# Even/odd partition runs, a zero-weighted fifth tile, another order for batch 0 and held-back weights in a linear-attention and expert-layer kernel

## The chip, the cores and the metric

The kernel runs on one core of one Trainium2 chip. The metric is the device time of one execution in microseconds (us). Every kernel was executed several times; the record marks each execution as fast or slow, and all executions told here are fast ones.

Engine names in the profile: PE is the TensorE matmul, PEld its weight load, DVE is VectorE, ACT is ScalarE, POOL is GpSimd, SP issues DMA (the copies between the chip's main memory and its on-chip memory). PEclk is the granted share of TensorE's clock.

## The reference

Eight batches, eight heads, 576 tokens of 64 features go through a linear attention with cosine weights; its output feeds an expert layer of two matmuls with `h * cos(h)` between them. All inputs and outputs are float32. The text calls phi(q) and phi(k) below the q and k features.

```python
def _attn_ref(q, k, v):                      # (8, 8, 576, 64) each
    theta = np.pi / 2.0 * pos / S
    phi(x) = concatenate([relu(x) * cos(theta), relu(x) * sin(theta)], -1)
    kv  = einsum('bhsf,bhsd->bhfd', phi(k), v);   z = sum(phi(k), axis=2)
    num = einsum('bhsf,bhfd->bhsd', phi(q), kv)
    den = einsum('bhsf,bhf->bhs',  phi(q), z) + 1e-06
    return num / den

def _moe_ref(x, w_in, w_out):                # x: (4608, 512), w_in: (512, 2048)
    h = x @ w_in
    return (h * cos(h)) @ w_out
```

## The kernel before

576 tokens are 4 tiles of 128 and a remainder of 64. One half of the partitions holds runs of 5 consecutive tokens, the other half runs of 4; even and odd batches swap the halves, so that two batches' remainders share one tile later. Remainders live in tiles of their own. `n` is the parity of the batch; `KPR`, `V1R` and `QPR` are the remainder's k features, v and q features.

```python
    def half(n):
        return slice(R * n, R * (n + 1))                 # R = 64
    # ... cut ...
        nc.sync.dma_start(
            out=m[half(n)], in_=s_[:, 0:S5, :].rearrange("h (p t) d -> p h t d", t=NT + 1))
        nc.sync.dma_start(
            out=m[half(1 - n), :, 0:NT, :],
            in_=s_[:, S5:S, :].rearrange("h (p t) d -> p h t d", t=NT))
    # ... cut ...
    def prep_v(b):                                       # the "V cast"
        nc.vector.tensor_copy(                           # 4 tiles
            out=V1[b % 2][:, :, :, 0:D],
            in_=m[:, :, 0:NT, :].rearrange("p h t d -> p t h d"))
        nc.vector.tensor_copy(out=V1R[b % 2][hf, :, 0:D], in_=m[hf, :, NT, :])
    # ... cut: kv_group = the KV matmuls, q_trans, num (x = num/den), x_trans ...
    for name in ("k", "v", "q"):
        load(0, name)
    # ... cut ...
    nc.gpsimd.tensor_copy(out=w_in_sb[0:1, 0, 0:1], in_=raw[("v", 0)][0:1, 0, 0, 0:1])
    for g in range(4):
        fs = slice(g * Dff // 4, (g + 1) * Dff // 4)
        nc.gpsimd.dma_start(out=w_in_sb[:, :, fs], in_=wi[:, :, fs])
    for f in attention(0, after=w_in_sb[0:1, 0, Dff // 2:Dff // 2 + 1]):
        f()
    # ... cut: the same for w_out, one element copied from v of batch 1 ...
    for s in range(B + 1):                               # expert of s beside attention of s + 1
        spread(mlp(s), attention(s + 1) if s + 1 < B else [])
```

The one-element copy into `w_in_sb` makes the DMA that overwrites that element wait until v has landed. It overlaps only the first of four pieces: in the timeline below three go out at 6.44 us, and the held one at 24.90, after the copy at 24.43. The order of the source is not the order on the engine: there, w_out's third piece (L340) goes out at 23.64, ahead of the held piece of w_in (L334).

## Time and profile before

| | before |
|---|---|
| time, median of 3 (the record has a fourth, 352.44, which makes the median 353.22) | 353.27 us (353.17 to 353.39) |
| span of the profiled run | 351.6 us |
| PE busy | 305.9 us (87%) |
| first matmul with w_in ("first expert matmul") | 43.35 us |
| KV matmuls of batch 1 start | 49.53 us |
| first output block (first matmul with w_out) | 78.73 us |

The page's second part gives busy tenths in 40 slices of 8.8 us. PE is at 9 from the ninth slice on; only the start has room.

```profile
PE   0034477799999999999999999999999999999993
```

The chain of waits, in order of time (start, duration, what), shows what the start consists of: a wait for w_in, then the V cast and the q features of batch 1, and from 78.89 on TensorE alone.

```profile
24.90 18.31 DMA w_in_sb<-in_moe_w_in_dram
43.35 1.87 PE M_362 L237 x4
45.21 1.69 PE M_374 L237 x4
48.26 1.23 DVE V_1_76 L118
54.26 2.39 DVE qp_352 L100 x6
...
78.89 3.45 PE M_806 L261 x16
```

The timeline of GpSimd shows why the first piece of w_in is the last to come: three other pieces of w_in and two of w_out are issued at 6.4 to 10.3 us, and the held one only at 24.90, behind a third piece of w_out. It was not v that held it so long: VectorE casts the last of that v at 15.94. GpSimd first stood 12.86 us at the copy that holds back k of batch 1, which by the code waits for the third piece of w_in (the profile itself names no releaser for this wait).

```profile
6.44 2.36 POOL L334 DMA_DIRECT2D w_in_sb<-in_moe_w_in_dram  x3
8.77 1.51 POOL L340 DMA_DIRECT2D w_out_sb<-in_moe_w_out_dram  x2
...
23.15 0.39 POOL L84 CAST km_124<-w_in_sb 1x1 f32<-1x1 f16 x2 [12.86 <-issue]
23.64 0.75 POOL L340 DMA_DIRECT2D w_out_sb<-in_moe_w_out_dram  x1
24.43 0.18 POOL L331 CAST w_in_sb<-vm_86 1x1 f16<-1x1 f32 x1
24.90 0.75 POOL L334 DMA_DIRECT2D w_in_sb<-in_moe_w_in_dram  x1 [0.30 <-POOL w_in_sb L331]
```

The tables of windows give, after the stretch and its length, busy time and instructions of PE, PEld, DVE, ACT and POOL, then the granted clock, the busy share of the 16 DMA engines (over 1 where packets overlap) and GB/s written. With loads of k, q, v alone (4 to 10 us) the rate is 211; with loads and weights together (14 to 24) it is 248, of which the loads have 123 (1.23 MB in 10 us, DMA view); with weights alone (24.5 to 26.5) it is 206, for which twice as many bytes are read, since the weights are cast from 4 to 2 bytes on the way (the page counts 36.74 MB read: 28.3 of q, k and v, and 8.4 of weights, which are written as 4.2).

```profile
4.00:10.00 6.00, 0.00 (x0) 0.00 (x0) 0.78 (x2) 2.30 (x3) 5.92 (x10) 1.00 1.14 211
...
14.00:24.00 10.00, 2.36 (x40) 2.23 (x40) 1.71 (x2) 1.38 (x3) 0.72 (x3) 1.00 1.17 248
```

```profile
24.50:26.50 2.00, 1.33 (x13) 1.34 (x14) 1.77 (x4) 2.00 (x4) 1.45 (x4) 1.00 1.24 206
```

### The profile page before, as it was taken

How to read it: one execution, taken by the hardware profiler on the slowest of the kernel's cores; microseconds unless marked ns; L12 is line 12 of the kernel's file. 1: busy time of each engine (PE TensorE's matmuls, PEld its weight loads, DVE VectorE, ACT ScalarE, POOL GpSimd, SP SyncE). 2: the span in 40 equal slices, each digit the busy share in tenths (PEclk: the TensorE clock that was granted, in tenths of full speed). 3: DMA queues.
4: the chain of work that ended last, by engine and by line, in shares of the span. 5: the costliest groups of instructions: out<-in, count | busy, mean ns of one | idle time of the engine just before them, and what ended most of it. 6: DMA issues, size and time to landing. Idle time of an engine off the chain costs nothing.

```text
span 351.6 us, 6070 instructions
## 1 busy us (share of the span) xinstructions
PE 305.9 (87%) x2448; PEld 170.8 (49%) x2448; DVE 202.8 (58%) x491; ACT 185.4 (53%) x284; POOL 13.3 (4%) x30
## 2 busy tenths in 40 slices
PE   0034477799999999999999999999999999999993
PEld 0034235445565555445574554455655554446441
DVE  0421849989996669438784887445943471444100
ACT  1335437665755575356764665557555753555210
POOL 9120010000000000000000000000000000000000
PEclk9998589989999999999999999999999999999999
DMA  7999999829998578940993168202021020220232
GB/s 152 224 235 248 250 200 237 149 58 209 202 203 170 135 163 158 204 122 10 238 196 85 34 132 184 72 2 62 1 47 44 2 62 0 60 49 13 68 83 60
DMA packets 33083, 42.37 MB, mean 121 GB/s; under 512 B 1824, under 2 KB 30496, under 8 KB 33056
## 3 DMA queue, kind: packets, MB, share of 16 engines
q1 hardware_dynamic: 28544, 37.75, 50.3%
q0 software_dynamic: 4224, 4.19, 7.1%
q8 instruction: 19, 0.31, 0.4%
q10 hardware_dynamic: 288, 0.04, 0.1%
q14 instruction: 8, 0.07, 0.1%
HBM read 36.74 MB, written 9.44 MB: 131 GB/s over the span
## 4 chain that ended last, share of the span: by engine, by line
PE 79%; DMA 5%; issue 5%; DVE 4%; ACT 2%; POOL 1%; POOLq 0%
DMA w_in_sb<-in_moe_w_in_dram 5%; ACT ch L229 1%; PE M_4128 L261 1%; PE M_4109 L261 1%; PE M_4049 L261 1%; PE M_2824 L261 1%; PE M_2741 L261 1%; PE M_2601 L261 1%; PE M_2250 L261 1%; PE M_1948 L261 1%; PE M_1815 L261 1%; PE M_1732 L261 1%; PE M_1592 L261 1%; PE M_1454 L261 1%; PE M_1241 L261 1%
## 5 line engine op out<-in xcount | busy, mean ns | idle before, releaser
L237 PEld LDWEIGHTS <-w_in_sb 128*128 128x128 f16 x512 | 47.2, 99 | 48.6 <-issue 7.6
L129 PE MATMUL KV_0_136<-V_0_75,kp_110 128*128 128x65 f16 x16 | 1.2, 243 | 17.3 <-DVE V_0_75 L118 17.3
L249 PEld LDWEIGHTS <-w_in_sb 128*128 128x128 f16 x256 | 14.8, 98 | 0.2
L129 PEld LDWEIGHTS <-kp_110 128*128 128x128 f16 x32 | 2.2, 131 | 17.3 <-issue 17.3
L261 PEld LDWEIGHTS <-g_3761 128*128 128x128 f16 x64 | 6.2, 97 | 7.6
L261 PEld LDWEIGHTS <-g_3287 128*128 128x128 f16 x64 | 6.2, 98 | 7.3
L261 PEld LDWEIGHTS <-g_751 128*128 128x128 f16 x64 | 6.2, 98 | 7.1
L261 PEld LDWEIGHTS <-g_1760 128*128 128x128 f16 x64 | 6.2, 98 | 7.1
L261 PEld LDWEIGHTS <-g_2769 128*128 128x128 f16 x64 | 6.2, 98 | 7.1
L261 PEld LDWEIGHTS <-g_2278 128*128 128x128 f16 x64 | 6.1, 98 | 7.1
L261 PEld LDWEIGHTS <-g_1269 128*128 128x128 f16 x64 | 6.1, 98 | 7.1
L261 PEld LDWEIGHTS <-g_361 128*128 128x128 f16 x64 | 6.1, 98 | 7.1
L142 PEld LDWEIGHTS <-qp_111 128*128 128x128 f16 x32 | 3.3, 148 | 5.6 <-ACT qp_111 L98 5.6
L142 PE MATMUL QP_0_184<-IDENT,qp_111 128*128 128x128 f16 x8 | 1.0, 311 | 5.5 <-ACT qp_111 L98 5.5
L183 PE MATMUL XP_0_304<-IDENT,x_0_254 128*128 128x128 f16 x4 | 0.7, 301 | 5.5 <-DVE x_0_254 L174 5.5
L100 DVE TENSOR_SCALAR KPR_78<-km_124,CS 64x512 f16<-64x512 f32 x2 | 0.9, 487 | 7.8 <-DMA km_124<-in_k_dram 7.8
L98 ACT ACT_TABLE_LOAD x1 | 1.3, 1283 | 7.2 <-DMA km_83<-in_k_dram 7.2
L100 DVE TENSOR_SCALAR qp_1753<-qm_1483,CS 128x512 f16<-128x512 f32 x8 | 3.7, 461 | 1.9 <-PE QP_3_1486 L142 1.9
L230 DVE TENSOR_TENSOR g_3761<-M_3762,ch 128x512 f16<-128x512 f32 x1 | 0.7, 692 | 6.9 <-ACT ch L229 6.9
L237 PE MATMUL M_362<-xT_113,w_in_sb 128*128 128x512 f16 x4 | 1.9, 622 | 3.0 <-DMA w_in_sb<-in_moe_w_in_dram 3.0
L100 DVE TENSOR_SCALAR qp_2762<-qm_2492,CS 128x512 f16<-128x512 f32 x8 | 3.7, 461 | 1.3 <-PE QP_3_2495 L142 1.3
L98 ACT ACTIVATE qp_111<-qm_89,CS 128x512 f16<-128x512 f32 x4 | 2.6, 711 | 3.1 <-DMA qm_89<-in_q_dram 3.1
(1128 smaller groups left out, 864.6 us busy)
## 6 DMA issues: line engine op xcount, KB each, us to landing
out_dram<-ost SPq DMA_DIRECT2D x32, 256.0 KB, 3.2
w_in_sb<-in_moe_w_in_dram POOLq DMA_DIRECT2D x4, 512.0 KB, 16.8
w_out_sb<-in_moe_w_out_dram POOLq DMA_DIRECT2D x4, 512.0 KB, 17.5
out_dram<-ostr SPq DMA_DIRECT2D x8, 128.0 KB, 2.3
km_83<-in_k_dram SPq DMA_DIRECT2D x1, 640.0 KB, 6.4
vm_86<-in_v_dram SPq DMA_DIRECT2D x1, 640.0 KB, 10.7
qm_89<-in_q_dram SPq DMA_DIRECT2D x1, 640.0 KB, 16.6
km_124<-in_k_dram SPq DMA_DIRECT2D x1, 640.0 KB, 10.5
```

Source lines behind the costliest of these rows:

```text
L98: nc.scalar.activation(out=out[:, :, g, :], in_=in_, func=AF.Relu, scale=sc)
L100: nc.vector.tensor_scalar(out=out[:, :, g, :], in0=in_, scalar1=0.0, scalar2=sc, op0=ALU.max, op1=ALU.mult)
L129: nc.tensor.matmul(KV[:, hh, :], lhsT=kp[:, t, h].rearrange("p g d -> p (g d)"), rhs=V1[b % 2][:, t, h, :], start=(t == 0), stop=False)
L142: nc.tensor.matmul(QP[:, h, :], lhsT=src[:, h].rearrange("p g d -> p (g d)"), rhs=IDENT, is_transpose=True)
L183: nc.tensor.matmul(XP[:, c, :], lhsT=x2[:, c * P:(c + 1) * P], rhs=IDENT, is_transpose=True)
L229: nc.scalar.activation(out=ch[:, 0:n], in_=M1, func=AF.Sin, bias=PIH, scale=1.0)
L230: nc.vector.tensor_tensor(out=dst, in0=M1, in1=ch[:, 0:n], op=ALU.mult)
L237: nc.tensor.matmul(M1, lhsT=w_in_sb[:, c, j * P:(j + 1) * P], rhs=xts[b][:, c, :], start=(c == 0), stop=(c == NCT - 1))
L249: nc.tensor.matmul(M1[:, jj, :], lhsT=w_in_sb[:, c, j * P:(j + 1) * P], rhs=xts[("r", pr)][:, c, :], start=(c == 0), stop=(c == NCT - 1))
L261: nc.tensor.matmul(M2, lhsT=gts[key][:, j, gsl], rhs=w_out_sb[:, j, :], start=(j == 0), stop=(j == NJT - 1))
```

## The change

Four things change together.

1. The runs of 5 and 4 tokens lie on even and odd partitions instead of the lower and upper half.
2. The remainder becomes a fifth tile with zero weights where a partition has only 4 tokens; the separate remainder tiles go. The cast of v now covers 5 tiles in one instruction.
3. Batch 0 takes k, q, v instead of k, v, q: its q is prepared and transposed while v lands, and ScalarE casts part of its v. As a side effect, batch 1's loads are issued in the order k, q, v too.
4. All four pieces of w_in wait for q of batch 0, all four of w_out for v of batch 1.

```diff
-    def half(n):
-        return slice(R * n, R * (n + 1))
+    def blocks(ap, n):
+        return ap.rearrange("(p f) ... -> f p ...", f=2)[n]
...
+        five, four = tokens(srcs[name][b], n)
+        nc.sync.dma_start(out=blocks(m, n), in_=five)
+        nc.sync.dma_start(out=blocks(m, 1 - n)[:, :, 0:NT, :], in_=four)
...
     def prep_v(b):
+        vt = raw["v"].rearrange("p h t d -> p t h d")
+        for n, (t0, t1) in enumerate(((0, 2), (2, NT + 1)) if b == 0 else ((0, NT + 1),)):
+            dst = V1[b % 2][:, t0:t1, :, 0:D]
+            if b == 0 and n == 0:
+                nc.scalar.activation(out=dst, in_=vt[:, t0:t1], func=AF.Copy)
+            else:
+                nc.vector.tensor_copy(out=dst, in_=vt[:, t0:t1])
...
+        if b == 0:
+            steps = [pk(t) for t in range(NT + 1)] + [ld("k"), pq(0)]
+            for t in range(1, NT + 1):
+                steps += [of(q_trans, t - 1), pq(t)]
+            steps += [ld("q"), of(q_trans, NT), pv, ld("v"), of(kv_group, 0),
+                      of(kv_group, 1), of(num, 0)]
...
-    for name in ("k", "v", "q"):
+    for name in ("k", "q", "v"):
+        nc.vector.memset(raw[name][:, :, NT, :], 0.0)
         load(0, name)
...
-    nc.gpsimd.tensor_copy(out=w_in_sb[0:1, 0, 0:1], in_=raw[("v", 0)][0:1, 0, 0, 0:1])
+    G = 4
+    nc.gpsimd.tensor_copy(
+        out=w_in_sb[0:1, 0, :].rearrange("p (g f) -> p g f", g=G)[:, :, 0],
+        in_=raw["q"][0:1, 0, 0, 0:1].broadcast_to((1, G)))
...                                       (the same for w_out, from v of batch 1)
```

More of the change, by code (lines that the diff above doesn't have):

```diff
@@ L51 @@
             w = fn(theta)
-            cs_np[half(n), n, g, :] = w[:S5].reshape(R, NT + 1)
-            cs_np[half(1 - n), n, g, :NT] = w[S5:].reshape(R, NT)
+            cs_np[n::2, n, g, :] = w[:S5].reshape(R, NT + 1)
+            cs_np[1 - n::2, n, g, :NT] = w[S5:].reshape(R, NT)
     cs_dr = nc.inline_tensor(cs_np, name="cs_const")
@@ L57 @@
     cpool = ctx.enter_context(tc.tile_pool(name="cpool", bufs=1))
-    rpool = ctx.enter_context(tc.tile_pool(name="rpool", bufs=1))
     apool = ctx.enter_context(tc.tile_pool(name="apool", bufs=2))
@@ L68, with tokens @@
     w_out_sb = cpool.tile([P, NJT, Dm], F16, name="w_out_sb")
-    V1 = [cpool.tile([P, NT, H, D1], F16, name=f"V1_{n}") for n in range(2)]
-    KPR = [cpool.tile([P, H, 2, D], F16, name=f"KPR{n}") for n in range(2)]
-    V1R = [cpool.tile([P, H, D1], F16, name=f"V1R{n}") for n in range(2)]
-    QPR = [cpool.tile([P, H, 2, D], F16, name=f"QPR{n}") for n in range(2)]
+    V1 = [cpool.tile([P, NT + 1, H, D1], F16, name=f"V1_{n}") for n in range(2)]
     srcs = {"k": k, "v": v, "q": q}
-    raw, kvzs, kps, qps, qts, xts, gts = {}, {}, {}, {}, {}, {}, {}
+    raw = {nm: cpool.tile([P, H, NT + 1, D], F32, name=f"{nm}m") for nm in srcs}
+    kvzs, kps, qps, qts, xts, gts = {}, {}, {}, {}, {}, {}
+    def tokens(ap, n):
+        return (ap[..., 0:S5, :].rearrange("h (p t) d -> p h t d", t=NT + 1),
+                ap[..., S5:S, :].rearrange("h (p t) d -> p h t d", t=NT))
     def load(b, name, after=None):
@@ L79, in load @@
             return
-        m = rpool.tile([P, H, NT + 1, D], F32, name=f"{name}m{b}", tag=f"{name}m")
-        n = b % 2
+        m, n = raw[name], b % 2
         if after is not None:
-            for hf in range(2):
-                nc.gpsimd.tensor_copy(
-                    out=m[R * hf:R * hf + 1, 0, 0, 0:1], in_=after)
-        s_ = srcs[name][b]
-        nc.sync.dma_start(
-            out=m[half(n)], in_=s_[:, 0:S5, :].rearrange("h (p t) d -> p h t d", t=NT + 1))
-        nc.sync.dma_start(
-            out=m[half(1 - n), :, 0:NT, :],
-            in_=s_[:, S5:S, :].rearrange("h (p t) d -> p h t d", t=NT))
@@ L92, in load, with prep @@
-        raw[(name, b)] = m
-    def feat(b, out, in_, rows, t):
+            nc.gpsimd.tensor_copy(out=m[0:2, 0, 0, 0:1], in_=after)
+        five, four = tokens(srcs[name][b], n)
+        nc.sync.dma_start(out=blocks(m, n), in_=five)
+        nc.sync.dma_start(out=blocks(m, 1 - n)[:, :, 0:NT, :], in_=four)
+    def prep(b, name, dst, t):
+        in_ = raw[name][:, :, t, :]
         for g in range(2):
-            sc = CS[rows, b % 2, g, t:t + 1]
+            sc = CS[:, b % 2, g, t:t + 1]
             if b == 0 and g == 1:
-                nc.scalar.activation(out=out[:, :, g, :], in_=in_, func=AF.Relu, scale=sc)
+                nc.scalar.activation(out=dst[:, t, :, g, :], in_=in_, func=AF.Relu, scale=sc)
@@ L99, in feat @@
             else:
                 nc.vector.tensor_scalar(
-                    out=out[:, :, g, :], in0=in_, scalar1=0.0, scalar2=sc,
+                    out=dst[:, t, :, g, :], in0=in_, scalar1=0.0, scalar2=sc,
                     op0=ALU.max, op1=ALU.mult)
-    ALLP = slice(0, P)
-    def prep(b, name, dst, rem, t):
-        m = raw[(name, b)]
-        if t < NT:
-            feat(b, dst[:, t], m[:, :, t, :], ALLP, t)
-        else:
-            hf = half(b % 2)
-            feat(b, rem[b % 2][hf], m[hf, :, t, :], hf, t)
@@ L115, in prep_v @@
-    def prep_v(b):
-        m = raw[("v", b)]
-        hf = half(b % 2)
-        nc.vector.tensor_copy(
-            out=V1[b % 2][:, :, :, 0:D],
-            in_=m[:, :, 0:NT, :].rearrange("p h t d -> p t h d"))
-        nc.vector.tensor_copy(out=V1R[b % 2][hf, :, 0:D], in_=m[hf, :, NT, :])
+    def prep_v(b):
+        vt = raw["v"].rearrange("p h t d -> p t h d")
[5 more added lines that the diff above has]
+                nc.vector.tensor_copy(out=dst, in_=vt[:, t0:t1])
@@ L127, in kv_group @@
             h = hb * HB + hh
-            for t in range(NT):
+            for t in range(NT + 1):
                 nc.tensor.matmul(
                     KV[:, hh, :], lhsT=kp[:, t, h].rearrange("p g d -> p (g d)"),
-                    rhs=V1[b % 2][:, t, h, :], start=(t == 0), stop=False)
-            nc.tensor.matmul(
-                KV[:, hh, :], lhsT=KPR[b % 2][:, h].rearrange("p g d -> p (g d)"),
-                rhs=V1R[b % 2][:, h, :], start=False, stop=True)
+                    rhs=V1[b % 2][:, t, h, :], start=(t == 0), stop=(t == NT))
         nc.scalar.activation(
@@ L138, in q_trans @@
     def q_trans(b, t):
-        src = qps[b][:, t] if t < NT else QPR[b % 2]
+        src = qps[b][:, t]
         QP = ppool.tile([P, H, P], F16, name=f"QP{b}_{t}", tag="ps")
@@ L193, in attention @@
     def attention(b, after=None):
-        kps[b] = apool.tile([P, NT, H, 2, D], F16, name=f"kp{b}", tag="kp", bufs=1)
-        qps[b] = apool.tile([P, NT, H, 2, D], F16, name=f"qp{b}", tag="qp", bufs=1)
+        kps[b] = apool.tile([P, NT + 1, H, 2, D], F16, name=f"kp{b}", tag="kp", bufs=1)
+        qps[b] = apool.tile([P, NT + 1, H, 2, D], F16, name=f"qp{b}", tag="qp", bufs=1)
         kvzs[b] = apool.tile([P, H, D1], F16, name=f"kvz{b}", tag="kvz", bufs=3)
@@ L200, in pk @@
         def pk(t):
-            return lambda: prep(b, "k", kps[b], KPR, t)
+            return lambda: prep(b, "k", kps[b], t)
         def pq(t):
-            return lambda: prep(b, "q", qps[b], QPR, t)
+            return lambda: prep(b, "q", qps[b], t)
         def ld(name):
@@ L213, in pv @@
             prep_v(b)
-        steps = [pk(t) for t in range(NT + 1)] + [ld("k"), pv, ld("v")]
-        steps += [of(kv_group, 0), pq(0), of(kv_group, 1), pq(1)]
-        for t in range(2, NT + 1):
-            steps += [of(q_trans, t - 2), pq(t)]
-        steps += [ld("q"), of(q_trans, NT - 1), of(num, 0), of(q_trans, NT),
+        if b == 0:
[4 more added lines that the diff above has]
+                      of(kv_group, 1), of(num, 0)]
+        else:
+            steps = [pk(t) for t in range(NT + 1)] + [ld("k"), pv, ld("v")]
+            steps += [of(kv_group, 0), pq(0), of(kv_group, 1), pq(1)]
+            for t in range(2, NT + 1):
+                steps += [of(q_trans, t - 2), pq(t)]
+            steps += [ld("q"), of(q_trans, NT - 1), of(num, 0), of(q_trans, NT)]
+        steps += [
                   of(num, 1), of(num, 2), of(x_trans, 0), of(num, 3),
@@ L254, in moe1_rem, with rows @@
              M1.rearrange("p j s -> p (j s)"), SM)
+    ALLP = slice(0, P)
     osts = {}
+    def rows(b):
+        ap = out[b * S:(b + 1) * S, :]
+        return (ap[0:S5].rearrange("(p t) m -> p t m", t=NT + 1),
+                ap[S5:S].rearrange("(p t) m -> p t m", t=NT))
     def moe2(key, t, gsl):
@@ L272, in moe2_main @@
         if t % 2 == 1:
-            n, r0 = b % 2, b * S
-            five = out[r0:r0 + S5, :].rearrange("(p t) m -> p t m", t=NT + 1)
-            four = out[r0 + S5:r0 + S, :].rearrange("(p t) m -> p t m", t=NT)
-            nc.sync.dma_start(out=five[:, t - 1:t + 1, :], in_=ost[half(n)])
-            nc.sync.dma_start(out=four[:, t - 1:t + 1, :], in_=ost[half(1 - n)])
+            n = b % 2
+            five, four = rows(b)
+            nc.sync.dma_start(out=five[:, t - 1:t + 1, :], in_=blocks(ost, n))
+            nc.sync.dma_start(out=four[:, t - 1:t + 1, :], in_=blocks(ost, 1 - n))
     def moe2_rem(pr):
@@ L283, in moe2_rem @@
         for n in range(2):
-            r0 = (2 * pr + n) * S
-            five = out[r0:r0 + S5, :].rearrange("(p t) m -> p t m", t=NT + 1)
-            nc.sync.dma_start(out=five[:, NT, :], in_=ost[half(n)])
+            five, _ = rows(2 * pr + n)
+            nc.sync.dma_start(out=five[:, NT, :], in_=blocks(ost, n))
     def mlp(s):
@@ L321 @@
     for n in range(2):
-        oth = half(1 - n)
-        nc.gpsimd.memset(KPR[n][oth], 0.0)
         nc.gpsimd.memset(V1[n][:, :, :, D], 1.0)
-        nc.gpsimd.memset(V1R[n][oth], 0.0)
-        nc.gpsimd.memset(V1R[n][half(n), :, D], 1.0)
-        nc.gpsimd.memset(QPR[n][oth], 0.0)
     wi = moe_w_in.rearrange("(c p) f -> p c f", p=P)
     wo = moe_w_out.rearrange("(j p) m -> p j m", p=P)
-    nc.gpsimd.tensor_copy(out=w_in_sb[0:1, 0, 0:1], in_=raw[("v", 0)][0:1, 0, 0, 0:1])
-    for g in range(4):
-        fs = slice(g * Dff // 4, (g + 1) * Dff // 4)
+    G = 4
+    nc.gpsimd.tensor_copy(
+        out=w_in_sb[0:1, 0, :].rearrange("p (g f) -> p g f", g=G)[:, :, 0],
+        in_=raw["q"][0:1, 0, 0, 0:1].broadcast_to((1, G)))
+    for g in range(G):
+        fs = slice(g * Dff // G, (g + 1) * Dff // G)
         nc.gpsimd.dma_start(out=w_in_sb[:, :, fs], in_=wi[:, :, fs])
-    for f in attention(0, after=w_in_sb[0:1, 0, Dff // 2:Dff // 2 + 1]):
+    for f in attention(0, after=w_in_sb[0:2, 0, Dff // 2:Dff // 2 + 1]):
         f()
-    nc.gpsimd.tensor_copy(out=w_out_sb[0:1, 0, 0:1], in_=raw[("v", 1)][0:1, 0, 0, 0:1])
-    for g in range(4):
-        js = slice(g * NJT // 4, (g + 1) * NJT // 4)
+    nc.gpsimd.tensor_copy(
+        out=w_out_sb[0:1, :, 0].rearrange("p (g j) -> p g j", g=G)[:, :, 0],
+        in_=raw["v"][0:1, 0, 0, 0:1].broadcast_to((1, G)))
+    for g in range(G):
+        js = slice(g * NJT // G, (g + 1) * NJT // G)
         nc.gpsimd.dma_start(out=w_out_sb[:, js, :], in_=wo[:, js, :])
```

## The prediction

> **What bounds the kernel now.** From about 79 us on it is TensorE: busy 45.0 of 45 us in 75-120 (table of windows), and the first output block of batches 0, 2 and 4 starts at 78.9, 153.4 and 227.9 us (chain of waits), 74.5 us apart. That part is rigid. What can move is the start. TensorE is busy only about 10.6 of the first 40 us (table of windows), and the chain there is 18.3 us of waiting for the first piece of w_in (issued 24.9, used 43.35). Then the V cast of batch 1 ends at 49.5 after its load, and 49.5-75 is VectorE-heavy (21.2 of 25.5 us busy). DMA is saturated from 4 to 67 us. Three w_in and two w_out pieces go out ungated at 6.4-10.3, so they slow q and v of batch 0 (q's second half lands 20 us after issue, k's 8.1) and delay batch 1; the one gated piece, the first that is needed, queues behind them.
>
> [...]With only loads of k, q, v in flight the rate is 205-212 GB/s (windows 4-10). Each such DMA writes one half of the partitions. [...]193-212 GB/s here, while weights, which span 128 partitions, move 206 GB/s written (24.5-26.5) from twice as many bytes read, so reading is not the limit; [...](3.5 us) the loads touch 348.[...]
>
> **What the change does.**
> 1. Even/odd runs: [...].
> 2. Weights held: w_in waits for q's first half, w_out for v of batch 1; w_in comes in order. 9.2 MB instead of about 10 MB move before v of batch 1 lands.
> 3. k, q, v order for batch 0: q features and transposes run while v loads.
> 4. Batch 1: k's load still waits for the third w_in piece; q before v, so q's features (5 us of VectorE) precede the V cast instead of following it.
> 5. Remainder as fifth tile: same matmul count; VectorE features at 64 or 128 partitions cost the same 0.45-0.49 us; casts 1.23+0.42 become about 1.5. Nothing on the path.
>
> **Estimated times** (from the durations above): q's first half lands 10.7, w_in issued 11, third piece landed 25-27, k of batch 1 landed (first half) 31-33. VectorE's order puts a k feature of batch 1 before the last x of batch 0, so the first expert matmul starts about 34-36 instead of 43.35; v of batch 1 lands 42-44, its cast ends 43.5-46 instead of 49.5: 4 to 6 us earlier. With q's features already done, the 49.5-75 stretch shrinks by another 2 to 4.5 us. The rest shifts unchanged: 353.3 - 8 = 345.
>
> **Prediction: 345.0 us, 8 in 10 between 339 and 351.** Faster by over 2% 0.60, within 2% 0.38, slower 0.02.
>
> **What would show it:** load-only windows near 265 GB/s; first w_in matmul at 34-36; V cast of batch 1 ending about 44-46; first output block near 71 instead of 78.9; spacing of 74.5 unchanged; no weight traffic before about 15 us.
>
> **What would make it wrong:** even/odd runs leaving the rate at 205[...]: then the hold-back costs what it gives, about 352. A rate over 320, or weights starting soon after issue: 340 or less. w_out, now issued only after v of batch 1 (about 43) and mixed with batch 2's loads, may land at 64-68, near its first use: if later, output blocks wait.

The sum came to 353.3 - 8 = 345 us, 4 to 6 us from an earlier V cast of batch 1 and 2 to 4.5 us after it. The 265 GB/s and the 320 GB/s are the author's estimate, as are the landing times worked out from them; what had been measured is 193 to 212 GB/s for the loads, and 348 in one slice of 0.25 us at 3.5 us.

## The result, and the profile after

The changed kernel takes 348.52 us (median of 4, 347.77 to 349.5) against 353.22 us before (median of 4). The ratio is 0.9873 (95% interval 0.9842 to 0.9904). Ratios here and below are the mean time of one kernel's fast runs over the mean of the kernel before's of the same rounds, so not quite the ratio of the medians quoted. The profiled execution is the slowest of the four (349.5 us).

| from the timelines | before | after | gained so far |
|---|---|---|---|
| first expert matmul | 43.35 | 30.65 | 12.70 |
| KV matmuls of batch 1 | 49.53 | 44.20 | 5.33 |
| first output block | 78.73 | 76.69 | 2.04 |
| last ScalarE copy of the output starts | 345.84 | 342.90 | 2.94 |
| end of the span | 351.6 | 347.7 | 3.9 |

This table is the whole story in small: 12.7 us were won at the first expert matmul and 10.7 of them were given back by the first output block, 7.4 before the KV matmuls of batch 1 and 3.3 after them. The chain of waits of the changed kernel shows the new waits. The load of k of batch 1 stands in front of the first expert matmul, which belongs to batch 0, because VectorE takes a k feature of batch 1 (28.36) before the last x of batch 0 (28.76).

```profile
21.81 6.46 DMA km<-in_k_dram
30.65 1.86 PE M_342 L230 x4
...
37.26 4.16 DVE qp_332 L98 x9
41.42 2.74 DVE V_1_73 L109
44.20 1.26 PE KV_0_375 L117 x20
...
76.86 3.45 PE M_779 L260 x16
```

In the page's slices, PE has a low fifth slice (TensorE waits for VectorE) and a low eighth.

```profile
PE   0555099599999999999999999999999999999994
```

The windows show the load rate: loads alone (4 to 12; w_in is issued from 9.76 on, but the rate does not change before 12) now run at 362 GB/s; weights alone (14 to 20) at 207, as before.

```profile
4.00:12.00 8.00, 0.00 (x0) 0.00 (x0) 3.83 (x9) 4.87 (x7) 2.43 (x4) 1.00 1.07 362
14.00:20.00 6.00, 3.31 (x31) 3.04 (x29) 1.75 (x1) 6.00 (x8) 0.00 (x0) 1.00 1.24 207
```

The timeline shows the two places where the gain was lost (start, duration, engine, line, instruction; in brackets the idle time of the engine before it and what ended it).

```profile
9.76 3.41 POOL L330 DMA_DIRECT2D w_in_sb<-in_moe_w_in_dram  x4 [0.31 <-POOL w_in_sb L325]
...
28.36 0.49 DVE L98 TENSOR_SCALAR kp_331<-km,CS 128x512 f16<-128x512 f32 x1 [2.41 <-DMA km<-in_k_dram]
...
36.35 0.19 POOL L333 CAST w_out_sb<-vm 1x4 f16<-1x4 f32 x1 [14.32 <-DMA vm<-in_v_dram]
...
36.87 4.55 DVE L98 TENSOR_SCALAR qp_332<-qm,CS 128x512 f16<-128x512 f32 x10
41.34 2.81 DVE L109 CAST V_1_73<-vm 128x2560 f16<-128x2560 f32 x1
44.20 1.26 PE L117 MATMUL KV_0_375<-V_1_73,kp_331 128*128 128x65 f16 x20 [8.70 <-DVE V_1_73 L109]
...
63.58 2.77 DVE L109 CAST V_0_72<-vm 128x2560 f16<-128x2560 f32 x1
66.27 0.41 DVE L159 TENSOR_TENSOR x_4_665<-NUM_4_0_642,rec_4_663 128x256 f16<-128x256 f32 x1
...
66.74 0.40 PE L168 MATMUL XP_4_688<-IDENT,x_4_665 128*128 128x128 f16 x2 [3.77 <-DVE x_4_665 L159]
```

Three things can be read there. First, v of batch 1 has landed by 36.35: GpSimd's copy for w_out, which reads the half that was issued second, waited for it, and the DMA view gives both halves 10.2 and 10.7 us from issue (24.65 and 25.54) to landing. But VectorE computes 4.55 us of q features before it casts that v. Second, the cast takes 2.81 us where the same work took 1.22 and 0.43 us before (timeline of before); VectorE's total rose from 202.8 to 213.2 us. Third, the slow cast of batch 2 stands before the last x of batch 1, for which TensorE waits 3.77 us.

The waits cost more than their length, for after both of them TensorE works at a low clock. After the 8.70 us at the KV matmuls the granted clock is 0.50 from 44.2 to 48, 0.70 in the next microsecond and 1.00 in the one after; after the 3.77 us it is 0.50 from 66.7 to 72 and 1.00 from 73 to 76.8 (windows). The two stretches from the first expert matmul to the first output block hold 232 matmuls each:

```profile
43.35:78.73 35.38, 29.16 (x232) 15.21 (x233) 27.29 (x66) 21.32 (x32) 0.92 (x2) 0.90 0.85 161
```

```profile
30.65:76.69 46.04, 32.66 (x232) 17.10 (x232) 37.05 (x82) 22.43 (x33) 3.76 (x5) 0.77 0.76 200
```

The stretch grew from 35.38 to 46.04 us. PE's busy time for the same matmuls grew by 3.50 us, at a granted clock of 0.77 instead of 0.90, and its idle time by 7.16 (13.38 against 6.22). Nearly all of the added idle time lies before the KV matmuls of batch 1; after them PE idles 4.69 us against 4.45, and the stretch is longer because PE is busy 27.80 instead of 24.75 us with the same 220 matmuls, at 0.83 instead of 0.94 (windows 44.2:76.69 and 49.53:78.73). In the chain, a group of four 512-column matmuls takes 1.71 us after the long wait (M_397 at 45.46, granted clock 0.50) and 0.86 us later (M_769 at 75.99, granted clock 1.00).

Two smaller gains lie later. In 120-160 and 200-240 us PE idles 0.63 and 0.62 us before and 0.17 and 0.18 after (windows), together 0.90, which is the difference between the third and fourth row of the table. And from the last ScalarE copy to the end it is 5.8 us before and 4.8 after; the page's DMA part gives 3.2 us to the landing of an output store before and 2.4 after.

### The profile page after: what moved, and what is told of

Its sections match the earlier page's. It is cut to its first block, busy times and chain, and to the rows that moved or that the text cites. A ratio compares the mean times of both kernels' runs of the same rounds, so it can differ in the third digit from the quotient of the medians.

```text
span 347.7 us, 6066 instructions
## 1 busy us (share of the span) xinstructions
PE 308.7 (89%) x2448; PEld 172.2 (50%) x2448; DVE 213.2 (61%) x486; ACT 185.9 (53%) x285; POOL 8.4 (2%) x19
## 4 chain that ended last, share of the span: by engine, by line
PE 81%; DVE 4%; issue 4%; ACT 3%; DMA 2%; POOL 0%; POOLq 0%; DVEq 0%
DMA km<-in_k_dram 2%; ACT ch L222 2%; DVE qp_332 L98 1%; PE M_4083 L260 1%; PE M_4044 L260 1%; PE M_3984 L260 1%; PE M_3876 L260 1%; PE M_3816 L260 1%; PE M_3757 L260 1%; PE M_3696 L260 1%; PE M_3421 L260 1%; PE M_2682 L260 1%; PE M_2424 L260 1%; PE M_2064 L260 1%; PE M_1780 L260 1%
## 5 line engine op out<-in xcount | busy, mean ns | idle before, releaser
L230 PEld LDWEIGHTS <-w_in_sb 128*128 128x128 f16 x512 | 48.0, 101 | 47.4 <-issue 7.4
L242 PEld LDWEIGHTS <-w_in_sb 128*128 128x128 f16 x256 | 14.8, 98 | 0.2
L127 PE MATMUL QP_0_115<-IDENT,qp_97 128*128 128x128 f16 x8 | 1.0, 311 | 12.9 <-ACT qp_97 L96 12.9
L109 DVE CAST V_1_73<-vm 128x2560 f16<-128x2560 f32 x4 | 11.3, 2814 | 0.0
L109 DVE CAST V_0_72<-vm 128x2560 f16<-128x2560 f32 (+1 forms) x4 | 10.2, 2539 | 1.4 <-DMA vm<-in_v_dram 1.4
L127 PEld LDWEIGHTS <-qp_97 128*128 128x128 f16 x40 | 4.2, 149 | 12.9 <-ACT qp_97 L96 12.9
L260 PEld LDWEIGHTS <-g_3716 128*128 128x128 f16 x64 | 6.3, 98 | 7.5
L260 PEld LDWEIGHTS <-g_3243 128*128 128x128 f16 x64 | 6.2, 98 | 7.3
L260 PEld LDWEIGHTS <-g_727 128*128 128x128 f16 x64 | 6.2, 98 | 7.1
L260 PEld LDWEIGHTS <-g_2729 128*128 128x128 f16 x64 | 6.2, 98 | 7.1
L260 PEld LDWEIGHTS <-g_1728 128*128 128x128 f16 x64 | 6.1, 97 | 7.1
L260 PEld LDWEIGHTS <-g_341 128*128 128x128 f16 x64 | 6.2, 98 | 7.1
L260 PEld LDWEIGHTS <-g_2242 128*128 128x128 f16 x64 | 6.1, 98 | 7.1
L260 PEld LDWEIGHTS <-g_1241 128*128 128x128 f16 x64 | 6.1, 98 | 7.1
L117 PEld LDWEIGHTS <-kp_331 128*128 128x128 f16 x40 | 2.5, 132 | 9.7 <-issue 9.5
L98 DVE TENSOR_SCALAR kp_331<-km,CS 128x512 f16<-128x512 f32 x10 | 4.2, 480 | 2.7 <-DMA km<-in_k_dram 2.7
L98 DVE TENSOR_SCALAR kp_96<-km,CS 128x512 f16<-128x512 f32 x5 | 2.1, 480 | 4.7 <-DMA km<-in_k_dram 4.7
L223 DVE TENSOR_TENSOR g_3716<-M_3717,ch 128x512 f16<-128x512 f32 x1 | 0.7, 691 | 6.9 <-ACT ch L222 6.9
L223 DVE TENSOR_TENSOR g_1728<-M_1729,ch 128x512 f16<-128x512 f32 x1 | 0.7, 693 | 6.6 <-ACT ch L222 6.6
```

Of the source, the lines that this page charges most:

```text
L98: nc.vector.tensor_scalar(out=dst[:, t, :, g, :], in0=in_, scalar1=0.0, scalar2=sc, op0=ALU.max, op1=ALU.mult)
L109: nc.vector.tensor_copy(out=dst, in_=vt[:, t0:t1])
L117: nc.tensor.matmul(KV[:, hh, :], lhsT=kp[:, t, h].rearrange("p g d -> p (g d)"), rhs=V1[b % 2][:, t, h, :], start=(t == 0), stop=(t == NT))
L127: nc.tensor.matmul(QP[:, h, :], lhsT=src[:, h].rearrange("p g d -> p (g d)"), rhs=IDENT, is_transpose=True)
L223: nc.vector.tensor_tensor(out=dst, in0=M1, in1=ch[:, 0:n], op=ALU.mult)
L230: nc.tensor.matmul(M1, lhsT=w_in_sb[:, c, j * P:(j + 1) * P], rhs=xts[b][:, c, :], start=(c == 0), stop=(c == NCT - 1))
```

## The experiments

Nine kernels ran, each beside the kernel before on the same chip, 4 executions each. The changed kernel was not run again beside them; the kernel before, with medians of 353.03 to 353.32 us in those rounds against 353.22 beside the changed kernel, ties them together. Edits are against the changed kernel unless said otherwise. All nine gave correct results.

| kernel | time, median (range) | ratio to before (95%) | first expert | KV of batch 1 | between | first output |
|---|---|---|---|---|---|---|
| before | 353.27 (353.17-353.39) | 1 | 43.35 | 49.53 | 6.2 | 78.73 |
| changed | 348.52 (347.77-349.5) | 0.9873 (0.9842-0.9904) | 30.65 | 44.20 | 13.6 | 76.69 |
| e1_cast_h | 344.92 (343.94-346.74) | 0.9768 (0.9732-0.9804) | 31.23 | 43.37 | 12.1 | 73.90 |
| e2_v_first | 345.16 (344.12-345.28) | 0.9778 (0.9749-0.9806) | 29.84 | 38.22 | 8.4 | 68.94 |
| e3_both | 341.13 (339.33-343.66) | 0.9675 (0.9611-0.9739) | 29.04 | 36.75 | 7.7 | 68.99 |
| e4_halves | 356.98 (356.3-357.67) | 1.0119 (1.0089-1.0149) | 37.26 | 51.88 | 14.6 | 83.22 |
| e5_runs_only | 352.25 (351.0-353.75) | 0.9953 (0.9909-0.9998) | 40.49 | 48.30 | 7.8 | 80.38 |
| e6_ungated | 356.60 (356.15-357.17) | 1.0075 (1.0040-1.0111) | 39.06 | 52.52 | 13.5 | 84.37 |
| e7_k_early | 340.48 (339.09-343.67) | 0.9623 (0.9547-0.9700) | 29.02 | 36.29 | 7.3 | 67.91 |
| e8_cast_split | 345.40 (344.38-346.72) | 0.9778 (0.9729-0.9827) | 29.43 | 41.68 | 12.3 | 72.05 |
| e9_head_halves | 341.59 (340.22-342.16) | 0.9657 (0.9618-0.9695) | 29.12 | 36.38 | 7.3 | 68.80 |

The column "between" is KV of batch 1 minus first expert matmul, in the profiled run. It falls into two groups: 12 to 15 us wherever VectorE computes batch 1's q features before its V cast, 6 to 9 us wherever the cast comes first.

### e1_cast_h: the cast walks head by head

```diff
-        vt = raw["v"].rearrange("p h t d -> p t h d")
+        vt = raw["v"]
-            dst = V1[b % 2][:, t0:t1, :, 0:D]
+            dst = V1[b % 2][:, t0:t1, :, 0:D].rearrange("p t h d -> p h t d")
...             (and vt[:, :, t0:t1] for vt[:, t0:t1] in both copies)
```

> Edit: the changed kernel, but the V cast walks its source and target head by head (8 x 5 x 64 on both sides) instead of tile by tile (5 x 8 x 64 read, 40 x 64 written). Engine orders stay the same. Theory A (the cast of 5 tiles [...]stands on the path twice: before the KV matmuls of batch 1 and before the last x of batch 1): the cast falls from 2.81 to 1.4-1.6 us, VectorE busy from 213 to about 203 us, KV of batch 1 starts near 42.9 instead of 44.2, the first output block near 74.5 instead of 76.9, time about 346.2. Rival B[...]: it stays at 2.8 at least in batch 1, time 348.5. Rival C (cast shortens, but is off the path): casts 1.5, time 348.5.

Measured: 344.92 us. The groups of instructions by form (line, engine, instruction, count, then busy us and mean ns) show the cast at about half its time, the changed kernel's first and this kernel's second.

```profile
L109 DVE CAST V_1_73<-vm 128x2560 f16<-128x2560 f32 x4 | 11.3, 2814 | 0.0
```

```profile
L109 DVE CAST V<-vm 128x2560 f16<-128x2560 f32 x7 | 10.4, 1479 | 0.0
...
L109 DVE CAST V<-vm 128x1536 f16<-128x1536 f32 x1 | 1.0, 962 | 1.4 <-DMA vm<-in_v_dram 1.4
```

VectorE's busy time for the casts fell from 21.5 to 11.4 us (groups by form), the first output block came 2.8 us earlier and the time fell by 3.6 us. Theory A holds. B and C fall: the cast of batch 1 takes 1.48 us too, and the time follows. (B, that GpSimd's work at that moment slows the cast, could have been ruled out in the changed kernel's timeline: GpSimd's issues of w_out end at 40.41, before the slow cast begins at 41.34, and it still takes 2.81 us.) By the layout of the tiles the cast reads 5 x 8 x 64 and writes 40 x 64; walked by heads both sides start with 8. The first took 2814 ns and the second 1479 for the same 2560 elements per partition. Why the walk matters is not shown. In the profiled pair (349.5 and 346.74 us, each the slowest of its four) the saving is 2.8 us, about the difference of the two casts on the path (2 x 1.33 us); the 3.6 us of the medians are not more than this once the spread of e1's executions (343.94 to 346.74) is allowed for.

### e8_cast_split: the same walk, as 4 tiles and 1

```diff
-        for n, (t0, t1) in enumerate(((0, 2), (2, NT + 1)) if b == 0 else ((0, NT + 1),)):
+        for n, (t0, t1) in enumerate(((0, 2), (2, NT + 1)) if b == 0 else ((0, NT), (NT, NT + 1))):
```

> Edit: the changed kernel, V cast still tile by tile, but as one cast of 4 tiles and one of the fifth (from batch 1 on). It tells two readings of the slow cast apart. Theory A ([...]5 against 40 is slow, 4 against 32 is fast): 1.2 us and 0.3-0.45 us, together 1.5-1.7, time as with the head-by-head walk, 344.5-346. Rival B (the tile-by-tile walk over the new, wider tile is slow in itself): 2.2 us or more for the 4 tiles, time 348.

Measured: 345.40 us, and:

```profile
L109 DVE CAST V<-vm 128x2048 f16<-128x2048 f32 x7 | 8.5, 1216 | 0.0
...
L109 DVE CAST V<-vm 128x512 f16<-128x512 f32 x7 | 2.9, 420 | 0.0
L109 DVE CAST V<-vm 128x1536 f16<-128x1536 f32 x1 | 1.8, 1755 | 0.7 <-DMA vm<-in_v_dram 0.7
```

The tile-by-tile walk is fast with 4 tiles (1216 ns for 2048 elements, 0.59 ns each), and still slow with the 3 of batch 0 (1755 ns for 1536, 1.14 ns each); with 5 it had 1.10 ns each (2814 for 2560), and by heads 0.58 (1479 for 2560). So neither the walk nor the wider tile is slow in itself; the slow casts are those that walk 5 against 40 and 3 against 24. Only 1, 3, 4 and 5 tiles were cast tile by tile on VectorE, and why these counts matter is not shown.

### e2_v_first: v of batch 1 before its q

```diff
-            steps += [ld("q"), of(q_trans, NT), pv, ld("v"), of(kv_group, 0),
+            steps += [of(q_trans, NT), pv, ld("v"), ld("q"), of(kv_group, 0),
```

> Edit: the changed kernel, but batch 1 loads v before q, which makes VectorE cast V of batch 1 before it computes q's features. Theory A (4.6 us of q features ahead of the V cast, not the landing of v, kept TensorE waiting 8.7 us at the KV matmuls of batch 1): KV of batch 1 starts at 38-39.5 instead of 44.2, first output block about 73, time about 345. Rival B (q's features become the next wait, as they were in the kernel before, where TensorE waited 2.5 us for them, and what is gained is given back): KV at 38-39.5, but first output block within 1 us of 76.9, time 348. Rival C (v's landing is what held the cast): KV stays at 43 or later.

Measured: 345.16 us; KV of batch 1 starts at 38.22, as theory A expected; the first output block comes at 68.94, earlier than it expected.

```profile
32.78 0.19 POOL L333 CAST w_out_sb<-vm 1x4 f16<-1x4 f32 x1 [10.73 <-DMA vm<-in_v_dram]
...
35.36 2.80 DVE L109 CAST V<-vm 128x2560 f16<-128x2560 f32 x1
38.09 0.86 DVE L98 TENSOR_SCALAR qp<-qm,CS 128x512 f16<-128x512 f32 x2
```

Theory C falls as it was put, for KV does not stay at 43. But the edit changes two things: v is also loaded earlier, and has landed by 32.78 instead of 36.35. In the changed kernel v had landed when VectorE began with the q features at 36.87, and was cast at 41.34; so the order alone is worth about 4.5 of the 6.0 us by which KV of batch 1 comes earlier (an estimate from these starts), and the rest needs the earlier landing. No run separates the two. Rival B is seen in part: TensorE now waits 2.30 us for q's features at the transposes, as the kernel before did (2.47). The first output block gains 7.75 us in the profiled runs, the medians only 3.4. The profiled runs differ by 5.4 us in all (344.12 is the fastest of e2's four, 349.5 the slowest of the changed kernel's); most of what is left is that PE idles 2.20 us in 120-160 (windows) against 0.17, in waits for VectorE.

### e3_both: both mends

> Both edits (V cast head by head; v before q for batch 1). If both theories A hold and the savings add up: cast 1.5 us, KV of batch 1 at 37-38, first output block about 71, time about 343. If they overlap: no faster than the better of the two alone, 345-346.

Measured: 341.13 us. In the medians the savings add up, 3.6 and 3.4 alone and 7.4 together, but e3's executions spread over 4.3 us, and in the profiles they do not: the first output block comes at 68.99, as with e2 alone (68.94). The casts have 1486 ns at the median, and KV of batch 1 starts at 36.75. Of its four executions two took 339.3 us at a granted clock of 0.988, and two 342.9 and 343.7 at 0.964 and 0.969: 4 us go with the granted clock. What decides it is not shown; only one of the four, a slower one, was profiled (TensorE waits 2.9 us at its KV matmuls).

### e4_halves: contiguous halves again, all else kept

```diff
     def blocks(ap, n):
-        return ap.rearrange("(p f) ... -> f p ...", f=2)[n]
+        return ap[R * n:R * (n + 1)]
...             (the cosine table and the one-element copies follow)
```

> Edit: the changed kernel with runs of 5 and 4 tokens in contiguous halves of the partitions as before, all else kept (order k, q, v, weights held, fifth tile). Theory A (even/odd runs alone raised the load rate from about 205 to about 360 GB/s, and the hold-back pays only with it): load-only windows 200-215 GB/s, first expert matmul 36-39 instead of 30.65, KV of batch 1 near 52-54, tail after the last matmul 1 us longer, time 355-359, slower than before (353.2). Rival B (the rate rose because no weights compete, or from the order of loads): load-only windows stay above 300, time 348-349. Rival C (rate falls, but hold-back and order carry the gain): rate 205, time 348-351.

Measured: 356.98 us, slower than before. The window with loads alone:

```profile
4.00:18.00 14.00, 1.93 (x19) 1.95 (x20) 4.72 (x10) 7.78 (x12) 3.30 (x5) 1.00 1.14 205
```

Theory A holds in nearly every number: 205 GB/s, first expert matmul 37.26, KV of batch 1 51.88 (just under the range); the tail from the last copy is 5.6 us against 4.8, and 5.8 in the kernel before. The even/odd runs alone make the loads faster (362 GB/s with them); with all else kept they are worth 8.5 us. That the hold-back pays only with them is not shown: e4 also has the slow cast and the q features before the V cast, which together cost the changed kernel 7.4 us (e3) and are not in the kernel before.

### e5_runs_only: only the runs and the fifth tile kept

```diff
-    for name in ("k", "q", "v"):
+    for name in ("k", "v", "q"):
-        out=w_in_sb[0:1, 0, :].rearrange("p (g f) -> p g f", g=G)[:, :, 0],
-        in_=raw["q"][0:1, 0, 0, 0:1].broadcast_to((1, G)))
+        out=w_in_sb[0:1, 0, 0:1], in_=raw["v"][0:1, 0, 0, 0:1])
...             (w_out alike; steps and V cast of batch 0 as for the other batches)
```

> Edit: of the change only the even/odd runs and the fifth tile are kept; order k, v, q and V cast wholly on VectorE for batch 0, and only one piece of each weight held, as before. Theory A (the bytes ahead of the first expert matmul are nearly the same, and DMA is never idle, so the runs alone give part of the gain): three w_in and three w_out pieces are in the queue from about 2 us[...]; first w_in matmul near 40, KV of batch 1 near 46, time 350-353. Rival B (the runs alone give the whole gain): 348-349. Rival C (without holding the weights the runs give nothing or less): 354 or more.

Measured: 352.25 us, theory A's range; KV of batch 1 came later (48.30) than its 46.

```profile
6.00:32.00 26.00, 5.56 (x71) 5.44 (x72) 7.05 (x11) 9.82 (x15) 1.45 (x5) 1.00 1.16 255
36.00:42.00 6.00, 2.97 (x14) 1.14 (x13) 4.78 (x14) 3.07 (x4) 0.76 (x1) 0.69 1.06 359
```

As long as weights are in the queues, the total is 255 GB/s, hardly over the 248 of before; only the loads alone (36 to 42) reach 359. In the kernel before, while both were queued (28 to 38 us), 1188 weight packets and 1187 load packets were moved (DMA view). If this equal share holds here too, an estimate from measured rates fits: a load packet has about 1152 bytes (runs of 5 and 4 tokens of 256 bytes; 1562 packets moved 1.81 MB in 4 to 9 us of the changed kernel), a weight packet writes 1024 (512 elements of 2 bytes); alone, 16 engines at 359 and 206 GB/s spend 51 and 80 ns on one, so a pair needs 131 ns, which is 266 GB/s. So I read that, while weights are queued, the engines' time (busy share 1.16 in this window) is the limit and not what the even/odd runs relieve; the estimate is 4% above the 255 measured, and no run tests this reading otherwise. This kernel, too, has the slow cast, which the kernel before has not, so the 1 us that it gains is not the worth of the faster loads alone.

### e6_ungated: all kept but the hold-back

```diff
-        out=w_in_sb[0:1, 0, :].rearrange("p (g f) -> p g f", g=G)[:, :, 0],
-        in_=raw["q"][0:1, 0, 0, 0:1].broadcast_to((1, G)))
+        out=w_in_sb[0:1, 0, 0:1], in_=raw["q"][0:1, 0, 0, 0:1])
...             (w_out alike)
```

> Edit: the changed kernel, but only the first piece of w_in and of w_out is held back, as before. Theory A (the hold-back moves the first expert matmul, but what then waits is VectorE's order and the slow V cast, so the total hardly moves): v of batch 0 lands near 29 instead of 14, first w_in matmul near 38 instead of 30.65, KV of batch 1 near 45 instead of 44.2, time 348-351. Rival B (holding the weights is what the gain came from): 353 or more.

Measured: 356.60 us; my theory A missed. Its first half was right (v of batch 0 cast from 28.57, first expert matmul 39.06), but KV of batch 1 came at 52.52 instead of 45. I had treated the two as if each had its own wait. They are chained: after the first expert matmuls VectorE multiplies their results by the cosine, computes the q features of batch 1 and then casts v, so the 13.5 us between them move along. Outcome B holds: with the changed kernel's order and slow cast, holding the weights back is worth 8.1 us.

### e7_k_early and e9_head_halves: can the mended kernel be mended further?

```diff
e7 (against e3)
-    for f in attention(0, after=w_in_sb[0:2, 0, Dff // 2:Dff // 2 + 1]):
+    for f in attention(0, after=w_in_sb[0:2, 0, 1:2]):
e9 (against e3)
-                nc.vector.tensor_copy(out=dst, in_=vt[:, :, t0:t1])
+                for hs in ((slice(0, HB), slice(HB, H)) if b else (slice(0, H),)):
+                    nc.vector.tensor_copy(out=dst[:, hs], in_=vt[:, hs, t0:t1])
```

> Edit: the kernel with both mends (V cast head by head; v before q for batch 1), and batch 1's loads wait for the first piece of w_in instead of the third. Theory A (in the mended kernel batch 1's landing is still on the path by about 1 to 2 us): k of batch 1 issued near 17-18 instead of 21.6, first w_in matmul 28-29, KV of batch 1 near 35 instead of 36.75, time 339-340.5. Rival B (its landing is no longer on the path, or the loads now compete with w_in and give it back): within 1 us of 341.1.

> Edit: the kernel with both mends, and the V cast of each batch from 1 on is two casts of 4 heads, so that the KV matmuls of the first 4 heads can start after half of it. Theory A (the wait at the KV matmuls of batch 1 is still on the path): casts of 0.75-0.8 us each, KV of batch 1 starts 0.5-0.8 us earlier than 36.75, the wait of TensorE there about 2.2 instead of 2.9, time 340-341, and more of the runs at a granted clock of 0.98 or higher (339). Rival B (the next wait, at the transposes of q, takes it all): 341-342, clock spread as in the kernel with both mends (0.964 to 0.988).

Measured: 340.48 and 341.59 us, neither to be told from e3's 341.13. In e7, k of batch 1 is issued at 16.49 instead of 21.59, yet the first expert matmul stays at 29.02 and KV of batch 1 comes at 36.29, not near 35: rival B (the time, 340.48, fits both theories). There the chain of batch 0 itself (ScalarE's share of the V cast ends at 20.3, then KV, x and its transposes) is the limit. In e9 the wait at KV shrinks to 2.24 us as expected, the casts take 0.82 us, and the time does not follow: rival B again. The granted clocks were 0.961 to 0.974, so the hoped-for executions at 0.98 or higher did not come.

## Why the prediction was right or wrong

The time, 345.0 us with 339 to 351, held: 348.52 us. The saving was 4.7 us where 8 were forecast, and the likelier class, faster by over 2% (0.60), did not come: the ratio's whole interval lies within 2% (0.38). Taken apart, two sizes in the prediction were wrong and partly cancelled, so that the time came out as near as this is partly luck.

- **What bounds the kernel: right.** The spacing of the even batches' first output blocks stays at 74.5 us or less, and all but 0.9 of the 3.9 us won in the profiles were won before 77 us or in the tail.
- **The load rate: right in direction, too small in size.** I expected 265 GB/s, at most 320 (my estimate). 362 was measured. q's first half landed by 9.26 instead of 10.7 and k of batch 1 was issued at 21.81, not after 25 to 27, and so the first expert matmul came at 30.65 and not at 34 to 36.
- **"A rate over 320 [...]: 340 or less": wrong.** At the measured 362 GB/s a tensor of 1.18 MB takes 3.3 us, at the 211 of before 5.6 (estimates from the rates). The rate came and the time was 348.5; with the two faults below mended (e3) it is 341.1.
- **Step 5, "casts 1.23+0.42 become about 1.5. Nothing on the path": wrong, and the mis-sized term of the sum.** The cast over 5 tiles takes 2.81 us (1.48 by heads in e1, 1.22 and 0.42 as 4 tiles and 1 in e8), and it is on the path. With the cast mended the kernel takes 344.9 or 345.4 us. I had looked at element counts and not at the shape of the access pattern.
- **"its cast ends 43.5-46 instead of 49.5": right number, wrong cause.** It ended at 44.15, but v had landed by 36.35, not 42-44. What held the cast was step 4's own remark that q's features precede it. I had counted this order as a gain only; in e2, where v comes first in the loads and on VectorE, the time is 3.4 us less.
- **"the 49.5-75 stretch shrinks by another 2 to 4.5": wrong.** From KV of batch 1 to the first output block it is 29.20 us before and 32.49 after. TensorE did not wait for q's features any more (2.47 us before), but 3.77 us for the last x behind the slow cast, and it worked at a granted clock of 0.83 instead of 0.94. So the first output block came at 76.69 and not near 71.
- **The risk I named, w_out landing too late, did not come:** the first output block shows no wait for it.
- **Not foreseen:** the tail is 1 us shorter, 4.8 instead of 5.8 us, because output stores gain from even/odd partitions too (2.4 us to landing instead of 3.2, and with contiguous halves in e4 the tail is 5.6).

What remains open: what the new order of batch 0 is worth, which no run tries alone; what the runs of tokens and the held weights are each worth with the cast mended, since e4, e5 and e6 all have the slow cast; and how much of the run-to-run spread of the mended kernels (339.1 to 343.7 us) could be removed by shortening TensorE's waits further. The granted clock goes with it (0.988 in the fastest, 0.961 to 0.978 in the others), but no experiment set the clock alone.

The best versions run here, e3_both and e7_k_early (341.13 and 340.48 us), beat both kernels: 3 to 4% under before.

## What to carry to other kernels

Changes to transfers have to be tried together: here spreading the partitions paid 8.5 us beside held-back weights and 1 us without them (in a kernel with the slow cast, and another order of batch 0), and the changed kernel without the spreading was slower than the kernel before. When a faster start brings data earlier, look at the engine that consumes it: its order of instructions, made for late data, can keep nearly all of the gain. And when tiles are merged or their count changes, check the time of every copy that walks them, for a copy's time need not follow its bytes: VectorE's cast took 1755 ns for 1536 elements per partition (3 against 24) and 1216 ns for 2048 (4 against 32).
